# Queries and keys of batch 2: from pair loads and TensorE transposes to token rows and DMA transposes

## The chip, the cores and the metric

The kernel runs on one NeuronCore of a Trainium2 chip. A core has five engines with a queue of instructions each: TensorE (PE in the profile; its weight loads are PEld), VectorE (DVE), ScalarE (ACT), GpSimd (POOL) and SyncE (SP, which here only issues DMAs). Each queue runs in order, and an instruction waits until the semaphores that it names have been raised. Sixteen DMA engines move data between HBM and the on-chip memory SBUF; SyncE issues to the queue that the profile calls q1, GpSimd to q0. TensorE writes to PSUM[...].

The metric is the device time of one execution in microseconds; smaller is better.

## What is computed

```python
scores = q @ k.T / sqrt(64)                      # batch 8, heads 8, sequence 576, head 64
c      = cumsum(max(s, 0))                       # per batch and head
scores = where(causal, -1e9, scores + min(-(c[i] - c[j]), 0))
attn   = softmax(scores)
x      = (attn @ v), heads side by side          # 8 x 576 x 512
out    = x + relu(layernorm(x) * g @ w1) @ w2    # w1 512 x 2048, w2 2048 x 512
```

Inputs and the output are float32; the kernel multiplies in bf16.

## The kernel before

**The work.** Attention goes head by head: the loop over `n` runs over 64 heads, n = 8b + h for head h of batch b. One pass of it is called a slot here. In slot n TensorE computes the transposed scores of head n in three PSUM banks (`sa`, `sb`, `sc`, L312) and, in every second slot, the last 64 x 64 block of two heads (`sd`, L347); ScalarE takes their exponentials into `er` (L323, L358). Heads from n = 10 on (`NM`) are masked afterwards by GpSimd, four selects a head on the diagonal blocks of `er` (L331) and one for two heads on the last block (L361). One slot later comes `pv` of head n-1: 15 small matmuls into `pot` (L389), and VectorE's division and copy into `xb` (L397 to L406). Between these pieces stand the "units" of the layer norm and MLP of an earlier batch: `mlp1`, four matmuls into `ph` (L497), and `mlp2`, quarters of four matmuls into `py` (L515). In slots 9 to 15 there are two units a slot, in slot 16 four, from slot 20 on about four.

**Queries and keys, two ways.** The scores need q and k with the head dimension on the partitions, in the tile `kq[i]`, i = group mod 2. A group `gam` is four heads, so batch b has groups 2b and 2b + 1. Four more partition rows hold the bias: -1 and c (in three bf16 parts), against c and ones, so that the matmul of depth 68 adds the bias itself.

The *pair way* is for batches below `NPE`. Two heads form a pair. `ld_cast_pair` (L130) has GpSimd issue two loads with a cast into bf16 (`kp`, `qp`, L128). `qk_pair` (L275) then has TensorE transpose the pair, six 96 x 96 transposes for k and six for q into two PSUM tiles `trqk` of the pool `ps_t` (L255), which `sd` and others also use, and VectorE and ScalarE copy them into `kq` (L100, L98). `aug` (L207) writes the bias rows with four small DMAs from SyncE.

The *row way* is for the other batches. `ld_rows` (L159) loads 128 token rows of four heads in float32, k and q in one DMA each from SyncE (128 KB each, `rowtmp`, L164). `cast_rows` (L172) has GpSimd cast them into one of four tiles `rows` (L176) and copy the bias columns beside them from `cT` (L177). `tr_rows` (L182) has SyncE issue a DMA transpose of the tile into `kq` (L186). A group has five tiles, the last of 64 rows. `cT` holds the bias by tokens; `bias_rows` (L232) fills it at slot 9 from the PSUM tile `trc`, and two memsets put its constants in. In the row way's layout a matmul over queries that pass the 512th is cut in two (`q_cols`, L289).

**What sets the order.** The program is written out by hand (`tc.manual_schedule()`, L68): each engine's queue is in the order of the Python calls. At the start of slot n, `pre(n)` (L675) issues what is to be in time for later slots. For group `gam`, with m = n - 4 gam, rows 0 and 1 are loaded at m = -6, cast at -5 while rows 2 and 3 are loaded, transposed at -4 while rows 2 and 3 are cast and row 4 is loaded, and so on to the last transpose at -2; the group's first head is at m = 0. The values of batch 2 (`vtmp`, L139) are loaded by SyncE in slots 11 to 15 and cast by GpSimd a slot later (L102). As `pre(n)` stands ahead of the scores, GpSimd's casts of a slot stand ahead of that slot's selects in its queue. The loads share six buffers of the pool `stage`, so that SyncE can issue them ahead of the slot that they are written in. The weights `w1` and `w2` come through GpSimd's queue with a cast: `w2` is issued in slots 7 and 10 (L201).

Of the kernel before, what the change touches and what calls it, by code (L numbers as in the profile page):

```python
# [19 lines left out]
def kernel(  # L20
# [11 lines left out]
    nc = tc.nc  # L32
# [13 lines left out]
    EW = 1664  # L46
    G = 4
    NG = BH // G
    NPE = 3
    NM = 10  # L50
    NR = 4
    QT = 6
# [33 lines left out]
    cT = const.tile([P, NT, 2, BH, 4], BF16, name="cT")  # L86
# [39 lines left out]
    def ld_cast(kind, g):  # L126
        ready[kind, g] = pair_tile(kind)
        nc.gpsimd.dma_start(out=ready[kind, g][0:QP], in_=pair_src(kind, g))  # L128

    def ld_cast_pair(g):  # L130
        ld_cast("k", g)
        ld_cast("q", g)
# [12 lines left out]
    def ld_cast_v(b, t):  # L145
        pn = P if t < NF else TL
        nc.gpsimd.dma_start(
            out=v_bf[b % 2][:pn, t, :, 0:D],
            in_=v[b, :, t * P : t * P + pn, :].rearrange("h s d -> s h d"),
        )  # L150
# [8 lines left out]
    def ld_rows(gam, t):  # L159
        pn = P if t < NF else TL  # L160
        b, h0 = gam // 2, (gam % 2) * G
        tmp = stage.tile([P, 2, G, D], F32, name="rowtmp", tag="st")
        for u, src in enumerate((k, q)):
            nc.sync.dma_start(  # L164
                out=tmp[0:pn, u],
                in_=src[b, h0 : h0 + G, t * P : t * P + pn, :].rearrange("h s d -> s h d"),
            )
        loaded["rows", gam, t] = tmp
# [27 lines left out]
    def ld_w1(c):  # L196
        sl = slice(c * 512, (c + 1) * 512)
        nc.gpsimd.dma_start(out=w1_bf[:, :, sl], in_=w1_r[:, :, sl])

    def ld_w2(i):  # L200
        nc.gpsimd.dma_start(  # L201
            out=w2_bf[:, 4 * i : 4 * i + 4, :], in_=w2_r[:, 4 * i : 4 * i + 4, :]
        )
# [3 lines left out]
    def aug(gam, eng, h0=0):  # L207
        r = slice(gam * G + h0, gam * G + G)
        i = gam % 2
        eng.dma_start(out=kq[i][D : D + 1, 1, h0:G, 0:S], in_=c_hi[r, :])  # L210
        for j in range(3):
            eng.dma_start(out=kq[i][D + 1 + j : D + 2 + j, 0, h0:G, 0:S], in_=c3[r, j, :])
# [19 lines left out]
    def bias_rows(tr):  # L232
        for t0, t1, pn in ((0, NF, P), (NF, NT, TL)):
            nc.vector.tensor_copy(
                out=cT[0:pn, t0:t1, 0, :, 1:4],
                in_=tr[0:pn, :, t0:t1, :].rearrange("p j t x -> p t x j"),
            )
            nc.vector.tensor_copy(out=cT[0:pn, t0:t1, 1, :, 0], in_=tr[0:pn, 0, t0:t1, :])
# [42 lines left out]
    def k_cols(b, h, kb):  # L281
        i, hh = (b * 2 + h // G) % 2, h % G
        if b < NPE:
            return kq[i][0:KA, 0, hh, kb * P : (kb + 1) * P]
# [4 lines left out]
    def q_cols(b, h, q0, q1):  # L289
        i, hh = (b * 2 + h // G) % 2, h % G  # L290
        if b < NPE:
            return [(q0, q1, kq[i][0:KA, 1, hh, q0:q1])]
# [374 lines left out]
    keep_warm(5)  # L667

    PAIR_LOADS = {11: 8, 12: 9, 13: 10, 16: 11}
    PAIRS = {9: 5, 11: 6, 13: 7, 14: 8, 15: 9, 16: 10, 21: 11}


    def pre(n):  # L675
        if n == 0:
            nc.vector.memset(mhalf, -0.5)
            ld_cast_pair(4)
        elif n == 1:
            ld_w1(1)  # L680
        elif n == 3:
            ld_cast_pair(5)
            for t in range(NT):
                ld_cast_v(1, t)
        elif n == 4:
            ld_w1(2)
            ld_w1(3)
        elif n == 7:
            ld_cast_pair(6)
            ld_w2(0)  # L690
            ld_cast_pair(7)
            ld_w2(1)
        elif n == 10:
            ld_w2(2)
            ld_w2(3)
        elif n == 12:
            nc.vector.memset(cT[:, :, 0, :, 0], -1.0)
            nc.vector.memset(cT[:, :, 1, :, 1:4], 1.0)
        elif n == 16:
            for r in rows:  # L700
                nc.gpsimd.memset(r[:, :, :, KA:P], 0.0)
        if n in PAIR_LOADS:
            ld_cast_pair(PAIR_LOADS[n])
        if n % 4 == 0 and 2 <= n // 4 + 1 < 2 * NPE:
            aug(n // 4 + 1, nc.sync)
        for gam in range(2 * NPE, NG):
            m = n - 4 * gam
            if m == -6:
                ld_rows(gam, 0), ld_rows(gam, 1)
            elif m == -5:  # L710
                cast_rows(gam, 0), cast_rows(gam, 1)
                ld_rows(gam, 2), ld_rows(gam, 3)
            elif m == -4:
                tr_rows(gam, 0), tr_rows(gam, 1)
                cast_rows(gam, 2), cast_rows(gam, 3)
                ld_rows(gam, 4)
            elif m == -3:
                tr_rows(gam, 2), tr_rows(gam, 3)
                cast_rows(gam, 4)
            elif m == -2:  # L720
                tr_rows(gam, 4)
        for nb in range(2, B):
            m = n - H * nb + (5 if nb == 2 else 7)
            if 0 <= m < NT:
                ld_v(nb, m)
            if 1 <= m <= NT:
                cast_v(nb, m - 1, "pool")
# [17 lines left out]
    for n in range(BH):  # L745
        b, h = n // H, n % H
        pre(n)
        if n < 8:
            scores(b, h)
            if h in (1, 3, 5, 6):  # L750
                scores_d(b, h // 2)
            if h in (0, 2, 4):
                qk_pair(h // 2 + 1, ("dve", "dve"), ("act", "dve" if h < 4 else "act"))
            pend.append((b, h))
            if n == 7:
                pv_next()
                tr_pair(4)
                pv_next()
                evac_pair("k", 4, ("act", "act"))
                evac_pair("q", 4, ("act", "act"))  # L760
                trc = bias_tr()
                keep_warm(8)
                continue
            if n % 2 == 1 or n == 0:
                keep_warm(2)
            if n > 1:
                pv_next()
            if n == 6:
                pv_next()
            continue  # L770
        if n == 8:

            phs = [
                pool.tile([P, 512], F32, name="ph", tag=tag)
                for pool, tag in ((ps_m, "m"), (ps_m, "m"), (ps_s, "s"), (ps_s, "s"))
            ]

            def columns(t):
                cols = slice(t * P, (t + 1) * P)
                for fb, ph in enumerate(phs):  # L780
                    for kd in range(KD):
                        nc.tensor.matmul(  # L782
                            ph[:, cols],
                            lhsT=w1_bf[:, kd, fb * P : (fb + 1) * P],
                            rhs=xTs[0][:, kd, cols],
                            start=(kd == 0),
                            stop=(kd == KD - 1),
                        )

            for t in range(NF):  # L790
                ln_tr(0, t, "act" if t < 3 else "dve")
                if t > 0:
                    columns(t - 1)
            columns(NF - 1)
            for fb, ph in enumerate(phs):
                if fb % 2 == 0:
                    nc.scalar.activation(out=hT[:, fb, :], in_=ph, func=ACT.Relu)
                else:
                    nc.vector.tensor_scalar_max(out=hT[:, fb, :], in0=ph, scalar1=0.0)
            ln_first_rstd()  # L800
            queue += batch_units(0)[4:]
            scores(b, h)
            scores_d(b, h // 2)
            pend.append((b, h))
            run_units(1)
            continue

        end = next(m for m in (8 * i + 3 for i in range(2, B + 1)) if m >= n)
        nu = (2 if n < 16 else -(-len(queue) // (end - n + 1))) - 2
        if n in PAIRS:  # L810
            qk_pair(PAIRS[n], ("dve", "dve"), ("act", "act"))
        scores(b, h)
        run_units(1, True)
        if h % 2 == 0:
            scores_d(b, h // 2)
        run_units(1)
        if n > 9:
            pv_next()
        if n == 9:
            bias_rows(trc)  # L820
        pend.append((b, h))
        lt = {2: (0, 1), 3: (2, 3, 4)}.get(h, ()) if b > 1 else ()
        for t in lt:
            ln_tr(b - 1, t, "act" if b == 2 else "dve")
            if t != 1 and t != 4:
                run_units(1)
                nu -= 1
        if n == 2 * H + 2:
            for t in range(3, NT):
                ln_xn(1, t)  # L830
        run_units(nu)
        if b > 1 and h == 3:
            run_units(len(queue))
            queue += batch_units(b - 1)
# [41 lines left out]
```

## Time and profile before

| What | Before |
|---|---|
| Time, median of 3 runs | 368.11 us (367.84 to 368.29) |
| Span of the profiled execution | 367.0 us |
| Instructions | 8372 |
| TensorE busy | 357.8 us, 97% |
| VectorE busy | 205.8 us, 56% |
| ScalarE busy | 194.2 us, 53% |
| GpSimd busy | 161.3 us, 44% |
| SyncE's DMA queue (q1) | 40.74 MB, 50.9% of 16 engines |
| GpSimd's DMA queue (q0) | 8.62 MB, 20.4% of 16 engines |

A busy share is the time in which the engine had at least one instruction under way, over the span. The time line of an engine lists its instructions by start and length, with the idle time before one and what ended it in brackets. The window view of the DMA queues gives, for a stretch of time, how many packets and bytes each queue moved. DMA share and busy time say nothing of who waits; that is read from the brackets and from the starts.

Some starts in the time line that the steps ahead use (in us from the start of the span): `sa` of slots 10 to 17 at 42.87, 46.69, 49.54, 53.13, 56.48, 61.12, 64.48 and 69.43; `sa` of slot 24 at 100.87. The transposes of pairs 7 to 11 start at 52.62, 55.97, 60.30, 63.96 and 86.36.

### The profile page before, as it was taken

The numbers are of one execution on the slowest core, as the hardware profiler recorded it, in microseconds if no ns is written. First come the engines' busy times: TensorE is split into PE (matmuls) and PEld (weight loads), VectorE is DVE, ScalarE is ACT, GpSimd is POOL, SyncE is SP. The second block draws the span as 40 slices with busy tenths as digits, with TensorE's granted clock in tenths as the row PEclk, the third lists the DMA queues.
The fourth block names the chain that finished last, engine by engine and source line by source line (L and its number), as shares of the span: only waits on it lengthen the run. The fifth ranks groups of instructions, "written<-read, shape, count | busy, mean of one in ns | idle before, by whom it ended". The sixth has DMA issues, their size and how long they took to land.

```text
span 367.0 us, 8372 instructions
## 1 busy us (share of the span) xinstructions
PE 357.8 (97%) x3079; PEld 198.0 (54%) x3079; DVE 205.8 (56%) x539; ACT 194.2 (53%) x371; POOL 161.3 (44%) x441
## 2 busy tenths in 40 slices
PE   8899999999999999999999999999999999999995
PEld 3577565565555555555555555555555554444444
DVE  7597789796438453944384547743675483112211
ACT  5795988568743674357534753476337522501410
POOL 8864375747553746445754562555652101000000
PEclk9999999999999999999999999999999999999999
DMA  7999995579965989599968996798730011011013
GB/s 138 170 195 175 201 204 88 116 179 173 187 140 129 236 177 189 117 227 184 192 158 203 206 188 133 183 202 183 167 102 2 0 60 57 3 56 58 3 29 86
DMA packets 147981, 50.42 MB, mean 137 GB/s; under 512 B 134185, under 2 KB 143268, under 8 KB 147940
## 3 DMA queue, kind: packets, MB, share of 16 engines
q1 hardware_dynamic: 129364, 40.74, 50.9%
q0 software_dynamic: 18176, 8.62, 20.4%
q10 hardware_dynamic: 400, 0.52, 0.5%
q8 instruction: 24, 0.39, 0.4%
q14 instruction: 17, 0.14, 0.2%
HBM read 37.11 MB, written 9.44 MB: 127 GB/s over the span
## 4 chain that ended last, share of the span: by engine, by line
PE 85%; DVE 7%; ACT 3%; DMA 2%; issue 1%; ACTq 0%
PE ph L497 32%; PE py L515 31%; PE pot L389 7%; PE sc L312 4%; PE sa L312 3%; PE sb L312 3%; DVE xn L451 2%; PE trx L484 2%; ACT er L323 2%; DMA kq<-c 1%; ACT kq L98 1%; PE trqk L255 1%; DVE stats L423 1%; PE ph L782 1%; DMA c_in<-in_s_dram 1%
## 5 line engine op out<-in xcount | busy, mean ns | idle before, releaser
L515 PE MATMUL py<-w_bf,hT 128*128 128x512 bf16 (+1 forms) x592 | 136.5, 373 | 0.4 <-DVE yo L524 0.4
L497 PE MATMUL ph<-xT,w_bf 128*128 128x512 bf16 x496 | 117.8, 379 | 0.1
L507 ACT ACTIVATE hT<-ph 128x512 bf16<-128x512 f32 x102 | 61.0, 598 | 62.8 <-PE ph L497 62.8
L515 PEld LDWEIGHTS <-hT 128*128 128x128 bf16 x592 | 53.5, 98 | 49.1 <-issue 0.9
L497 PEld LDWEIGHTS <-w_bf 128*128 128x128 bf16 x560 | 50.3, 97 | 51.7 <-issue 3.3
L323 ACT ACTIVATE er<-sa 128x512 bf16<-128x512 f32 x64 | 38.2, 597 | 70.3 <-PE sa L312 39.9
L331 POOL TENSOR_SCALAR_AFFINE_SELECT er<-er 128x128 bf16<-128x128 bf16 x216 | 58.2, 294 | 26.4 <-ACT er L323 26.3
L505 DVE TENSOR_SCALAR hT<-ph 128x512 bf16<-128x512 f32 x38 | 26.3, 692 | 54.5 <-PE ph L497 49.1
L176 POOL CAST rows<-rowtmp 128x512 bf16<-128x512 f32 (+1 forms) x50 | 30.5, 609 | 49.1 <-DMA rowtmp<-in_q_dram 48.4
L312 PEld LDWEIGHTS <-kq 68*128 68x128 bf16 x440 | 32.8, 97 | 26.5 <-DMA kq<-c 1.6
L389 PEld LDWEIGHTS <-er 128*128 128x128 bf16 x960 | 37.4, 98 | 14.2 <-issue 0.7
L389 PE MATMUL pot<-v_bf,er 128*128 128x65 bf16 x960 | 39.6, 193 | 0.1
L323 ACT ACTIVATE er<-sc 128x512 bf16<-128x512 f32 x64 | 39.1, 610 | 0.0
L397 DVE RECIPROCAL rinv<-pot 128x5 f32<-128x5 f32 x64 | 12.3, 192 | 47.5 <-PE pot L389 47.2
L323 ACT ACTIVATE er<-sb 128x512 bf16<-128x512 f32 x64 | 38.3, 598 | 0.1
L524 DVE SCALAR_TENSOR_TENSOR yo<-py,rstd,xb 128x512 f32<-128x512 f32 x32 | 23.9, 748 | 25.5 <-PE py L515 20.8
L399 DVE TENSOR_TENSOR xb<-pot,rinv 128x256 f32<-128x256 f32 x64 | 27.2, 425 | 2.2
L439 POOL TENSOR_TENSOR rstd<-rstd,mhalf 128x4 f32<-128x4 f32 (+1 forms) x8 | 8.8, 1097 | 43.8 <-DVE rstd L438 43.8
L312 PE MATMUL sa<-kq 68*128 68x512 bf16 x64 | 24.4, 381 | 1.2 <-DMA kq<-c 1.1
L423 DVE BATCH_NORM_STATS2 stats<-xb 128x6 f32<-128x128 f32 (+2 forms) x100 | 25.3, 312 | 0.4
L312 PE MATMUL sc<-kq 68*128 68x256 bf16 (+1 forms) x208 | 25.2, 232 | 0.3
L102 POOL CAST v_bf<-vtmp 128x512 bf16<-128x512 f32 (+1 forms) x30 | 18.4, 613 | 14.3 <-DMA vtmp<-in_v_dram 14.3
(101 smaller groups left out, 332.8 us busy)
## 6 DMA issues: line engine op xcount, KB each, us to landing
out_dram<-yo SPq DMA_DIRECT2D x32, 256.0 KB
vtmp<-in_v_dram SPq DMA_DIRECT2D x24, 256.0 KB
rowtmp<-in_k_dram SPq DMA_DIRECT2D x40, 128.0 KB
rowtmp<-in_q_dram SPq DMA_DIRECT2D x40, 128.0 KB
w_bf<-in_moe_w_ch_dram POOLq DMA_DIRECT2D x8, 512.0 KB, 11.1
kp<-in_k_dram POOLq DMA_DIRECT2D x11, 144.0 KB, 6.6
qp<-in_q_dram POOLq DMA_DIRECT2D x11, 144.0 KB, 7.3
v_bf<-in_v_dram POOLq DMA_DIRECT2D x8, 128.0 KB, 8.5
```

The source lines that it names most:

```text
L176: nc.gpsimd.tensor_copy(out=r[0:pn, :, :, 0:D], in_=loaded.pop(("rows", gam, t))[0:pn])
L312: nc.tensor.matmul(a[:, c + a0 - q0 : c + a1 - q0], lhsT=k_cols(b, h, kb), rhs=cols, start=True, stop=not (pe_mask and diag),)
L323: nc.scalar.activation(out=e[:, o : o + 512], in_=a, func=ACT.Exp, scale=scale)
L331: nc.gpsimd.affine_select(out=e[:, o : o + P], in_=e[:, o : o + P], compare_op=ALU.is_ge, fill=0.0, base=0, pattern=[[1, P]], channel_mult ...
L389: nc.tensor.matmul(pot[:, t, :], lhsT=e[:, o : o + P], rhs=vv[:, kb, h, :], start=(kb == 0), stop=(kb == last),)
L399: nc.vector.tensor_tensor(out=xb[b][:, :, hs], in0=pot[:, 0:NF, 0:D], in1=rinv[:, 0:NF].unsqueeze(2).to_broadcast([P, NF, D]), op=ALU.mult,)
L423: nc.vector.bn_stats(out=st[b][:, t, part, :], in_=x[:, lo:hi])
L497: nc.tensor.matmul(ph, lhsT=w1_bf[:, kd, fb * P : (fb + 1) * P], rhs=xT[:, kd, :], start=(kd == 0), stop=(kd == KD - 1),)
L505: nc.vector.tensor_scalar_max(out=hT[:, fb, :], in0=ph, scalar1=0.0)
L507: nc.scalar.activation(out=hT[:, fb, :], in_=ph, func=ACT.Relu)
L515: nc.tensor.matmul(py[0], lhsT=hT[:, fb, t * P : (t + 1) * P], rhs=w2_bf[:, fb, c0:c1], start=(fb == 0), stop=(fb == FB - 1),)
L524: nc.vector.scalar_tensor_tensor(out=yo, in0=py[0], scalar=rs, in1=x[:, c0:c1], op0=ALU.mult, op1=ALU.add)
```

## The change

Batch 2 goes from the pair way to the row way. `NPE` is 2 in place of 3, so that groups 4 and 5 come from `ld_rows`, `cast_rows` and `tr_rows` in slots 10 to 18, and scores of batch 2 read the row layout. Pairs 8 to 11 go from the tables of loads and transposes; pairs 5 to 7 stay, with loads in slots 3 and 7 that the diff doesn't touch. The two `aug` calls of groups 4 and 5 (slots 12 and 16) drop out by the bound on `n // 4 + 1`. As `cast_rows` now needs `cT` in slot 11, its two memsets come ahead of `bias_rows` in slot 9, and the zeroing of the four tiles `rows` moves from slot 16 to slot 10. The purpose is to take batch 2's transposes from TensorE and their evacuations from VectorE and ScalarE, and to use the DMA path that batches 3 to 7 already have.

```diff
-    NPE = 3
+    NPE = 2
...
-    PAIR_LOADS = {11: 8, 12: 9, 13: 10, 16: 11}
-    PAIRS = {9: 5, 11: 6, 13: 7, 14: 8, 15: 9, 16: 10, 21: 11}
+    PAIRS = {9: 5, 11: 6, 13: 7}
...
         elif n == 10:
             ld_w2(2)
             ld_w2(3)
-        elif n == 12:
-            nc.vector.memset(cT[:, :, 0, :, 0], -1.0)
-            nc.vector.memset(cT[:, :, 1, :, 1:4], 1.0)
-        elif n == 16:
             for r in rows:
                 nc.gpsimd.memset(r[:, :, :, KA:P], 0.0)
-        if n in PAIR_LOADS:
-            ld_cast_pair(PAIR_LOADS[n])
...
         if n == 9:
+            nc.vector.memset(cT[:, :, 0, :, 0], -1.0)
+            nc.vector.memset(cT[:, :, 1, :, 1:4], 1.0)
             bias_rows(trc)
```

## The prediction

> **What bounds the kernel now.** I read the shares first, then the chain that ended last, then the time line of slots 12 to 16 engine by engine, then the DMA queues by window. A slot is one head, n = 8b+h; its scores start with the `sa` matmul.
>
> ```profile
> PE 357.8 (97%) x3079; PEld 198.0 (54%) x3079; DVE 205.8 (56%) x539; ACT 194.2 (53%) x371; POOL 161.3 (44%) x441
> ...
> PE 85%; DVE 7%; ACT 3%; DMA 2%; issue 1%; ACTq 0%
> ```
>
> TensorE is the bound, so a change pays by what it takes from TensorE's queue and costs what it makes that queue wait for. In the time line, TensorE's part of slots 13 to 15:
>
> ```profile
> 52.87 0.42 PE L255 MATMUL trqk<-ident,qp 96*128 96x96 bf16 x6
> 53.13 0.38 PE L312 MATMUL sa<-kq 68*128 68x512 bf16 x1
> ...
> 55.51 0.62 PE L389 MATMUL pot<-v_bf,er 128*128 128x65 bf16 x15
> 55.97 0.42 PE L255 MATMUL trqk<-ident,kp 96*128 96x96 bf16 x6
> 56.22 0.42 PE L255 MATMUL trqk<-ident,qp 96*128 96x96 bf16 x6
> 56.48 0.38 PE L312 MATMUL sa<-kq 68*128 68x512 bf16 x1
> ...
> 58.56 0.22 PE L347 MATMUL sd<-kq 68*128 68x64 bf16 x2 [0.40 <-ACT kq L98]
> ```
>
> The 12 transposes of a pair take 0.51 us (55.97 to 56.48), and their evacuation then holds up `sd`. The `pot` at 55.51 is PV of head 12; it needs that head's four causal selects (L331), which GpSimd issues in order behind the casts of the same slot:
>
> ```profile
> 52.52 1.04 POOL L331 TENSOR_SCALAR_AFFINE_SELECT er<-er 128x128 bf16<-128x128 bf16 x4
> 53.52 0.29 POOL L361 TENSOR_SCALAR_AFFINE_SELECT er<-er 64x128 bf16<-64x128 bf16 x1
> ...
> 55.23 0.61 POOL L102 CAST v_bf<-vtmp 128x512 bf16<-128x512 f32 x1 [0.19 <-DMA vtmp<-in_v_dram]
> ```
>
> So head 12's selects end at 53.6, 1.9 us before PV wants them, and a cast at the head of GpSimd's queue does wait for its DMA. Last, the queues in 34 to 40 us, when SyncE's queue (q1) holds one load, the values of batch 2, tile 0, issued at 30.30:
>
> ```profile
> DMA packets 2000, 1.17 MB, mean 195 GB/s; under 512 B 1013, under 2 KB 1999, under 8 KB 1999
> q0 software_dynamic: 1034, 0.90, 91.5%
> q1 hardware_dynamic: 965, 0.25, 30.8%
> ```
>
> That one load of 256 KB, 1024 packets of 256 B, needs those six microseconds: while GpSimd's queue (q0: weights, pairs) has a backlog, the queues get packets one for one, and q1's are small.
>
> [...] Here the window 86 to 102 us, six transposes among row loads, moved this much[...]:
>
> ```profile
> DMA packets 11261, 2.84 MB, mean 177 GB/s; under 512 B 11256, under 2 KB 11256, under 8 KB 11257
> ```
>
> [...]
>
> **The change part by part.**
>
> *TensorE work removed.* Pairs 8 to 11 (slots 14, 15, 16, 21): 4 x 0.51 = 2.05 us. Their waits go too: slot 14 lasts 3.82 us from `sa` to the next transposes, against 3.08 for slot 12, which has no pair: 0.74. In slot 15 the transposes take 0.82, not 0.51: 0.31. In slot 16 `sd` comes 1.20 us after the first unit starts, against 0.86 in slot 12: 0.34. Sum 3.44 us. The eight evacuations on DVE and eight on ACT (0.80 each) lie beside TensorE and pay only through those waits.
>
> *TensorE work added.* Batch 2's scores take the split layout, three more small matmuls a head. From `sa` to the next unit it is 0.65 us in slot 16 (pair layout, 64.48 to 65.13) and 0.66 in slot 24 (row layout): 8 x 0.01, nothing.
>
> *DVE, two memsets at slot 9.* 0.33 + 0.86 us ahead of `bias_rows`. PV of head 9 waits for its bank and comes at 45.73; `bias_rows` ended at 44.77, so 1.2 us more would reach about 46.0: up to 0.2 us, taken as 0.1.
>
> *GpSimd.* The four row memsets (1.81 us) move to slot 10, where GpSimd idled 3.05 us: nothing. Eight pair issues at 0.64 go (5.1 us); ten casts at 0.61 and ten bias copies at 0.21 come (8.2 us). It is 44% busy; busy time is not the cost, waiting is.
>
> *The new wait.* After the two old `aug` calls SyncE's next instructions are the rows of group 4, tiles 0 to 3: eight loads, 4 x 1024 packets, issued from 30.3 on, ahead of the values. They meet the same backlog. From 34 to 49 us q0 moved 1034 + 1931 = 2965 packets (second number: window 40 to 49). Shared at 172 a us (1034/6) those last to 34 + 17.2 = 51.2. Meanwhile q1 gets 161 a us: 2770 packets. Left are 1326 of rows and 1024 of values. Alone, q1 moved 11257 packets in 16 us, 704 a us: 3.3 us, to 54.5. From last packet to release I take 1.4 us (the completions of the load issued at 30.30 end at 41.7, its packets near 40.3): 55.9. Cast 0.6, four selects 1.04: head 12's selects end at 57.6, later if the slowest of the 16 engines lags. PV wants them at 55.5: a wait of 2.1 us or more.
>
> Behind that, each slot's selects stand behind the cast of the next load, and q1 carries transposes too (a 128-row tile 1024 packets, like its load). At 704 a us: two transposes, the half tile and values 1 (3584 packets) end at 59.6, so head 13's selects at 62.6; TensorE, 3.1 us after its last PV began (0.46 + 2.63 as in slot 12), asks at 60.7: 1.9. Two transposes and values 2 (3072) end at 64.0, selects at 67.0; asked at 65.4 (0.46 + 2.38 as in slot 13): 1.6. Half a transpose, two tiles of group 5 and values 3 (3584) end at 69.1, selects at 72.1; asked at 70.1: 2.0. The next slots are longer and GpSimd catches up. Sum 7.6 us. All five transposes of group 4 land by about 66, when slot 16 starts near 67.5: no wait of their own.
>
> *Both ends of the unknown rate.* Row loads alone can run near the pace at which SyncE issues them, 512 packets in 0.51 to 0.56 us, some 950 a us. The same steps then give waits of 1.2, 0.7, 0.4 and 0.7: 3.0 us. At 600 a us, below any such window here, they give 2.7, 2.8, 2.3 and 2.9: 10.7 us. I take 704, since transposes are in the mix, and that slowest engine is not in it.
>
> *Removed at no gain.* Pair loads leave q0 after 49 us, when w2 is nearly in; two `aug` calls, eight small DMAs, were in time already.
>
> Net: -3.4 + 0.1 + 7.6 = +4.3; shaded for a rate above 704 where loads alone are queued, +4: 372.0 us.
>
> **The rivals.**
> 1. *The rows come in time* and TensorE keeps all 3.4 us: 364.7. For it: in batches 3 to 7 the same path starves GpSimd for 48.4 us of waits for rows, yet TensorE is at 9 tenths nearly throughout. Against it: slots 22 to 24 last 4.6 us each, slots 11 to 15 3.6 on average (46.69 to 64.48), and q0 is empty there.
> 2. *Waits and savings cancel*: the 950 end, 368.1 - 3.4 + 3.0 = 367.7, or up to 368.5. For it: loads in isolation run at that pace. Against it: five transposes in the stretch.
> 3. *Worse*: at 600 a us, 368.1 - 3.3 + 10.7 = 375.5[...]: taken as 376.5. [...]
>
> **How the numbers follow.** Forecast 0.60, rival 1 0.17, rival 2 0.10, rival 3 0.13. The range runs from below rival 2, 366.5, to 377.5, leaving out rival 1 and the far end of rival 3. Faster by over 0.2% (under 367.4): rival 1 and a little of rival 2, 0.19. Within 0.2%: 0.05. Slower: 0.76.
>
> **What would show it.** No `trqk` after slot 13; q1 holding 4 x 1024 row packets in 34 to 54 us at one for one with q0; GpSimd's L176 waiting for `rowtmp` in 50 to 56 us; head 12's selects after 56.5; gaps on TensorE ahead of `pot` L389 in slots 13 to 16, put down to POOL `er` L331. I am wrong if L331 of head 12 ends before 55.5: then the sharing of the queues was misread and rival 1 holds.

## The result and the profile after

The changed kernel takes 372.41 us (median; 371.49 to 372.76), the kernel before 368.20 us beside it: a ratio of 1.0108, 95% interval 1.0083 to 1.0133. It is slower, by about 4.2 us.

The page of the kernel after, its lines for the shares, the DMA engines in 40 slices, the two queues and the chain that ended last:

```profile
PE 359.1 (97%) x3055; PEld 196.9 (53%) x3055; DVE 200.4 (54%) x531; ACT 188.4 (51%) x363; POOL 168.6 (45%) x453
...
DMA  8999999999997999689988989699730011011013
...
q1 hardware_dynamic: 148372, 45.43, 58.4%
q0 software_dynamic: 16512, 7.44, 17.1%
...
PE 63%; DMA 15%; SPq 8%; DVE 6%; POOL 4%; issue 2%; ACT 1%; POOLq 0%; ACTq 0%
```

TensorE has 24 matmuls fewer (48 transposes of pairs out, 24 small score matmuls in) and yet is "busy" for longer; its clock, at half for 3.4 us, explains that below. The line that tells the story is the last: DMA and SyncE's queue (SPq) hold 23% of the chain of work that ended last, where DMA held 2% before.

Where the 4 us lie is read from the starts of `sa`, slot by slot. The column "bare" is a run that is told of further down, without the rows of group 4.

| Slot length, us | before | after | bare |
|---|---|---|---|
| 10 | 3.82 | 4.58 | 4.59 |
| 13 | 3.35 | 2.84 | 2.84 |
| 14 | 4.65 | 3.93 | 3.07 |
| 15 | 3.35 | 5.27 | 2.84 |
| 16 | 4.96 | 7.86 | 4.63 |
| 20 | 5.14 | 4.63 | 4.63 |
| 21 | 4.81 | 4.57 | 4.57 |
| 24 | 4.63 | 5.04 | 4.63 |
| 10 to 24 together | 62.64 | 66.70 | 59.75 |

From 62.64 to 66.70 is +4.06, about the difference of the two profiled executions (spans of 367.0 and 371.1 us). The slots between that are not listed agree within 0.02. Outside these slots two small differences nearly cancel: this execution came to slot 10 by 0.69 us sooner, in a start that differs from execution to execution, and lost 0.6 us after slot 24.

What the change spares is 3.65: 62.64 - 59.75 = 2.89, and 0.76 more because slot 10 is longer. What it costs is 0.76 in slot 10 and 66.70 - 59.75 = 6.95 in slots 14, 15, 16 and 24.

TensorE's time line, after (start, length, engine, line, operation, and in brackets the idle time before it and what ended it):

```profile
45.79 0.63 PE L389 MATMUL pot<-v_bf,er 128*128 128x65 bf16 x15 [0.57 <-DVE cT L238]
...
58.94 1.20 PE L389 MATMUL pot<-v_bf,er 128*128 128x65 bf16 x15
59.98 0.38 PE L312 MATMUL sa<-kq 68*128 68x512 bf16 x1
...
64.03 1.11 PE L389 MATMUL pot<-v_bf,er 128*128 128x65 bf16 x15 [1.50 <-POOL er L331]
65.25 0.38 PE L312 MATMUL sa<-kq 68*128 68x512 bf16 x1
67.01 0.57 PE L312 MATMUL sb<-kq 68*128 68x64 bf16 x3 [1.39 <-DMA kq<-rows]
...
67.83 1.90 PE L515 MATMUL py<-w_bf,hT 128*128 128x512 bf16 x4
```

From slot 10 on the `pot` of slot n is PV of head n - 2: slots 8 and 9 add their heads to the list and run no PV, so the lag is two slots and not the one that the description of the kernel before gives. The `pot` at 58.94 and at 64.03 are those of heads 12 and 13.

Read the lengths too. A `pot` of 15 matmuls takes 0.6 us; those at 58.94 and 64.03 take 1.2 and 1.1, because the selects that they wait for come one by one while it runs, and that part of the wait stands in no bracket. The four `py` matmuls at 67.83 take 1.90 in place of 1.03: half the clock, which this line of the view by windows shows (the PEclk is the third figure from the end; it was 1.00 in the windows on both sides):

```profile
67.10:70.50 3.40, 3.40 (x16) 1.52 (x17) 0.82 (x2) 1.36 (x3) 2.73 (x9) 0.50 1.01 228
```

By estimate, 3.40 us at a clock of 0.50 cost 1.7 us, and no idle time is to be seen: TensorE counts as busy for all 3.40. A run that is told of further down, with the clock at full (run 2), bears this out: from `sb` of slot 16 to `sa` of slot 17 it takes 4.42 us there (66.53 to 70.95) and 6.09 here (67.01 to 73.10).

GpSimd's time line, after, says why the selects are late:

```profile
53.84 0.61 POOL L176 CAST rows<-rowtmp 128x512 bf16<-128x512 f32 x1 [3.04 <-DMA rowtmp<-in_q_dram]
...
56.31 0.61 POOL L176 CAST rows<-rowtmp 128x512 bf16<-128x512 f32 x1 [1.71 <-DMA rowtmp<-in_q_dram]
...
58.03 0.62 POOL L102 CAST v_bf<-vtmp 128x512 bf16<-128x512 f32 x1 [0.95 <-DMA vtmp<-in_v_dram]
58.59 1.04 POOL L331 TENSOR_SCALAR_AFFINE_SELECT er<-er 128x128 bf16<-128x128 bf16 x4
...
63.12 0.61 POOL L102 CAST v_bf<-vtmp 128x512 bf16<-128x512 f32 x1 [0.91 <-DMA vtmp<-in_v_dram]
63.68 1.03 POOL L331 TENSOR_SCALAR_AFFINE_SELECT er<-er 128x128 bf16<-128x128 bf16 x4
```

Three casts wait for their DMA, and head 12's selects, which need none of these data, stand behind them: they end at 59.6 (53.6 before). Head 13's stand behind the cast of values 1, at 63.12, and end at 64.7. The DMA queues of the kernel after in 34 to 51 us, and then in 51 to 73:

```profile
q0 software_dynamic: 2828, 2.57, 90.9%
q1 hardware_dynamic: 2829, 0.70, 31.5%
```

```profile
q1 hardware_dynamic: 15358, 3.82, 91.7%
q0 software_dynamic: 356, 0.34, 9.2%
```

In 34 to 51 us, while w2 has a backlog, it is one packet for one (2829 of q1, 2828 of q0), and q1 gets 0.70 MB against 2.57. In 51 to 73 us q1 moves 15358 packets, 698 a us in the mean, but not evenly. The share of the DMA engines in this stretch, in 40 slices of 0.55 us, is in the first line that of the kernel after, in the second that of the kernel before:

```profile
DMA  9999986599416994454999997999799999999998
...
DMA  7999999999999953000000000000000599999943
```

Before, the engines stand idle for some 8 us of it. After, they are busy but for gaps near 57 and from 59 to 61.5 us; from 58 to 74 us q1 moves 13040 packets, 815 a us. Around those gaps SyncE's time line has

```profile
49.22 8.92 SPq L186 DMA_TRANSPOSE kq<-rows  x2
...
59.63 0.61 SPq L139 DMA_DIRECT2D vtmp<-in_v_dram  x1
```

The first two transposes hold SyncE for 8.92 us, and the load of values 1 is issued behind them, at 59.63.

### The profile page after: what moved, and what is told of

Its sections match the earlier page's. It is cut to its first block, busy times and chain, and to the rows that moved or that the text cites. A ratio compares the mean times of both kernels' runs of the same rounds, so it can differ in the third digit from the quotient of the medians.

```text
span 371.1 us, 8359 instructions
## 1 busy us (share of the span) xinstructions
PE 359.1 (97%) x3055; PEld 196.9 (53%) x3055; DVE 200.4 (54%) x531; ACT 188.4 (51%) x363; POOL 168.6 (45%) x453
## 3 DMA queue, kind: packets, MB, share of 16 engines
q1 hardware_dynamic: 148372, 45.43, 58.4%
## 4 chain that ended last, share of the span: by engine, by line
PE 63%; DMA 15%; SPq 8%; DVE 6%; POOL 4%; issue 2%; ACT 1%; POOLq 0%; ACTq 0%
PE py L515 26%; PE ph L497 23%; SPq L164 6%; DMA rowtmp<-in_q_dram 6%; PE pot L389 5%; DMA kq<-rows 3%; DMA vtmp<-in_v_dram 3%; PE sb L312 2%; PE sc L312 2%; PE sa L312 2%; DVE xn L451 2%; POOL er L331 1%; DMA kq<-c 1%; PE trx L484 1%; POOL rows L176 1%
## 5 line engine op out<-in xcount | busy, mean ns | idle before, releaser
L515 PEld LDWEIGHTS <-hT 128*128 128x128 bf16 x592 | 53.6, 98 | 49.6 <-issue 2.1
L331 POOL TENSOR_SCALAR_AFFINE_SELECT er<-er 128x128 bf16<-128x128 bf16 x216 | 60.8, 307 | 17.5 <-ACT er L323 17.5
L176 POOL CAST rows<-rowtmp 128x512 bf16<-128x512 f32 (+1 forms) x60 | 36.7, 612 | 65.1 <-DMA rowtmp<-in_q_dram 61.9
L312 PEld LDWEIGHTS <-kq 68*128 68x128 bf16 x464 | 34.0, 98 | 29.4 <-DMA kq<-rows 3.3
L389 PEld LDWEIGHTS <-er 128*128 128x128 bf16 x960 | 37.6, 98 | 17.8 <-POOL er L331 2.6
L389 PE MATMUL pot<-v_bf,er 128*128 128x65 bf16 x960 | 40.8, 194 | 2.3 <-POOL er L331 1.5
L397 DVE RECIPROCAL rinv<-pot 128x5 f32<-128x5 f32 x64 | 12.3, 193 | 53.3 <-PE pot L389 53.0
L312 PE MATMUL sb<-kq 68*128 68x384 bf16 (+2 forms) x176 | 24.7, 244 | 2.0 <-DMA kq<-rows 1.6
```

The source lines that it names most:

```text
L176: nc.gpsimd.tensor_copy(out=r[0:pn, :, :, 0:D], in_=loaded.pop(("rows", gam, t))[0:pn])
L312: nc.tensor.matmul(a[:, c + a0 - q0 : c + a1 - q0], lhsT=k_cols(b, h, kb), rhs=cols, start=True, stop=not (pe_mask and diag),)
L331: nc.gpsimd.affine_select(out=e[:, o : o + P], in_=e[:, o : o + P], compare_op=ALU.is_ge, fill=0.0, base=0, pattern=[[1, P]], channel_mult ...
L389: nc.tensor.matmul(pot[:, t, :], lhsT=e[:, o : o + P], rhs=vv[:, kb, h, :], start=(kb == 0), stop=(kb == last),)
L515: nc.tensor.matmul(py[0], lhsT=hT[:, fb, t * P : (t + 1) * P], rhs=w2_bf[:, fb, c0:c1], start=(fb == 0), stop=(fb == FB - 1),)
```

## The experiments

Each run changes the changed kernel, unless it says otherwise; a ratio is to the kernel before, measured beside it (368.13 us beside runs 1 to 4, 368.41 beside 5 to 7 and 10, 368.22 beside 8 and 9). Theory A is that of the prediction: the data come late because the DMA queues are full, and the waits of TensorE only pass this on; each expectation says what follows from it in that run.

**1. The constants sooner.** `cT`'s constants and the zeroes of `rows` are written by GpSimd in slot 8.

```diff
+        elif n == 8:
+            nc.gpsimd.memset(cT[:, :, 0, :, 0], -1.0)
+            nc.gpsimd.memset(cT[:, :, 1, :, 1:4], 1.0)
+            for r in rows:
+                nc.gpsimd.memset(r[:, :, :, KA:P], 0.0)
```

> The changed kernel, with the two memsets of cT and the four of rows put on GpSimd in slot 8, where it waited 4.5 us for the statistics. Theory A (DMA data of group 4 come late; the memsets only cost the 0.57 us that PV waits for the bank of trc in slot 10): the wait in slot 10 goes and the time falls by 0.5 to 0.8 us, to about 371.7. Theory B (the later waits have slack of their own and swallow it, since the DMA chain sets slots 14 to 16 by absolute time): slot 10 is shorter by 0.7 us, but slots 14 to 16 are longer by as much, and the time stays at 372.4.

Measured: 373.31 us, ratio 1.0142 (1.0122 to 1.0161), above what either theory gave; of the two, theory B of this run is the nearer. Slot 10 is back to 3.82 us, so its 0.76 us were the memsets. But their removal bought nothing: slots 15 and 16 take 4.01 and 9.14 us. `sa` of slot 17 starts at 73.63, against 73.10 after, although TensorE reached slot 16 sooner:

```profile
64.49 0.38 PE L312 MATMUL sa<-kq 68*128 68x512 bf16 x1 [0.23 <-DMA kq<-rows]
...
66.21 0.61 PE L312 MATMUL sb<-kq 68*128 68x64 bf16 x3 [1.34 <-DMA kq<-rows]
```

The last transposes still land when slot 16 has begun. The clock was then halved (PEclk 0.50) for two windows, 65.6 to 72.4, in place of one, which made it worse than after. (This profile comes to slot 10 by 2.1 us later than the one after, and it had a halved window earlier too, PEclk 0.50 in 14.4 to 17.8 us; its starts are to be read with that in mind.)

**2. TensorE kept busy.** Seven matmuls on zeroes go ahead of PV in slot 15 and ahead of the scores in slot 16, where it waited.

```diff
+        if n == 16:
+            keep_warm(7)
...
+        if n == 15:
+            keep_warm(7)
```

> The changed kernel, with seven idle matmuls of 512 columns (1.5 us) ahead of PV in slot 15 and seven ahead of the scores of slot 16, where TensorE waits anyway. Theory A (1.7 us of the loss is the halved clock after these waits): the granted clock stays at 1.0 and the time falls by 1.5 to 2 us, to about 370.6. Rival (the half clock is hidden behind the DMA chain, or comes from elsewhere): the time stays at 372.4 or rises by up to 3 us of idle matmuls.

Measured: 372.66 us, ratio 1.0118 (1.0104 to 1.0132): theory A's 370.6 missed, the rival's 372.4 came. The clock stays full (a mean of 1.0 in the profiled execution, 0.995 after), slot 16 takes 5.17 us, and `sa` of slot 17 comes at 70.95, 2.15 us sooner than after. Then it is given back, wait by wait:

```profile
78.17 0.74 PE L389 MATMUL pot<-v_bf,er 128*128 128x65 bf16 x10 [0.43 <-POOL er L331]
...
85.28 0.38 PE L312 MATMUL sb<-kq 68*128 68x64 bf16 x3 [0.45 <-DMA kq<-rows]
...
104.93 0.40 PE L312 MATMUL sb<-kq 68*128 68x64 bf16 x3 [1.09 <-DMA kq<-rows]
```

At slot 25 it is 0.5 us behind after. So in this run the full clock alone buys nothing: what it gains comes back as waits for selects and for `kq`. That the packets of the DMA queues make these later waits was not shown.

**3. Half of w2.** The second half of `w2` is not loaded, and the first half is used twice (the output is then not that of the reference).

```diff
-            ld_w2(2)
-            ld_w2(3)
...
-                rhs=w2_bf[:, fb, c0:c1],
+                rhs=w2_bf[:, fb % 8, c0:c1],
```

> The changed kernel without the loads of the second half of w2, its first half used twice (that part of the computation is left out). 1 MB, 1024 packets of GpSimd's queue, are taken out of the backlog in which the rows of group 4 are loaded. Theory A (the DMA engines are full from the start to 74 us, and the rows get one packet for each packet of GpSimd's queue): group 4's rows land by 50 us, the waits of slots 14 to 16 go or fall below 1 us in all, and the time is 364.5 to 367. Rival (GpSimd's 8 us of added casts and copies, or the DMA transposes themselves, make the waits): 371 to 372.4.

Measured: 365.87 us, ratio 0.9944 (0.9933 to 0.9955). Nothing of the row path was touched, and all its waits up to slot 23 are gone. GpSimd's line for the selects of head 12, which end at 53.3 as before the change:

```profile
52.25 1.04 POOL L331 TENSOR_SCALAR_AFFINE_SELECT er<-er 128x128 bf16<-128x128 bf16 x4
```

`sa` of slot 17 starts at 66.12, 6.98 us sooner than after; 0.49 of this was there at slot 11. This is theory A. In the profiled execution about half is lost again at slot 24 (8.18 us in place of 4.63), where TensorE, now early, waits for group 6 and drops to half the clock (two windows of the kernel with half of w2, the second with PEclk 0.50). That execution is the slowest of 20, 368.64 us with a mean clock of 0.994; the other 19 have 0.998 or more, so the halved window is its own:

```profile
98.96 0.39 PE L312 MATMUL sb<-kq 68*128 68x64 bf16 x3 [1.73 <-DMA kq<-rows]
```

```profile
96.60:100.00 3.40, 1.67 (x13) 0.77 (x12) 0.34 (x2) 1.81 (x5) 1.85 (x6) 1.00 1.21 127
100.00:103.40 3.40, 3.40 (x25) 1.84 (x23) 0.00 (x0) 0.81 (x3) 2.35 (x8) 0.50 1.37 219
```

**4. Rows for group 5 alone.** Group 4 keeps its pairs, so that the first rows are wanted four slots later.

```diff
+    NPG = 5
...
-        if b < NPE:
+        if b * 2 + h // G < NPG:
...
-    PAIRS = {9: 5, 11: 6, 13: 7}
+    PAIR_LOADS = {11: 8, 12: 9}
+    PAIRS = {9: 5, 11: 6, 13: 7, 14: 8, 15: 9}
```

> Half of the change: group 4 stays on the pair way, group 5 takes the row way (loads from slot 14 on). Theory A (only the loads that meet the backlog of GpSimd's queue cost; group 5's come after it): no wait for rows or casts on TensorE, pairs 10 and 11 with their waits saved (about 1.6 us), 0.7 us lost to the memsets in slot 9: 367.0 to 367.6 us. Rival (the row way costs GpSimd or DMA time in itself): half of the loss, about 370.

Measured: 367.68 us, ratio 0.9979 (0.9963 to 0.9996): slightly faster than before, just above theory A's span. No wait for rows is left in slots 10 to 24; slot 10 keeps its 0.58 us for `cT`. Group 5's rows cost TensorE nothing; group 4's, asked for in the stretch of w2, do.

**5. The selects ahead of the casts.** Before slot 20 GpSimd casts a slot's rows and values after the slot's selects.

```diff
+    late = []
+    def behind(n, f, *a):
+        if n < 20:
+            late.append(lambda: f(*a))
...
-                cast_rows(gam, 0), cast_rows(gam, 1)
+                behind(n, cast_rows, gam, 0), behind(n, cast_rows, gam, 1)
```

> The changed kernel, but for slots before 20 GpSimd gets the casts of rows and values behind the slot's causal selects in place of ahead of them. Nothing is loaded sooner. Theory A (the row data is late because the DMA queues are full from 34 to 73 us; GpSimd's order only passes the lateness on): the waits for selects in slots 14 and 15 go (0.84 and 2.43 us), but the transposes of group 4 can't start sooner, so that slot 16 takes the lateness over as one wait of its sb for kq of 3 to 5 us, with the clock halved behind it: sa of slot 17 at 72 to 74 (after: 73.10), time 371.5 to 373.5. Rival C (the lateness is made by GpSimd's queue, in which selects stand behind a cast that waits): the waits of slots 14 and 15 go and nothing takes their place, 369 to 370.

Measured: 373.29 us, ratio 1.0113 (1.0077 to 1.0149), as theory A said (`sa` of slot 17 at 74.44, a little past its 72 to 74). TensorE's PV no longer waits, and the scores of slot 16 do, for longer:

```profile
62.12 0.62 PE L389 MATMUL pot<-v_bf,er 128*128 128x65 bf16 x15
...
65.50 0.38 PE L312 MATMUL sa<-kq 68*128 68x512 bf16 x1 [2.76 <-DMA kq<-rows]
...
67.14 0.60 PE L312 MATMUL sb<-kq 68*128 68x64 bf16 x3 [1.26 <-DMA kq<-rows]
```

The last transpose lets `sb` go at 67.14; after, it was 67.01. GpSimd's order decides in which bracket the wait stands, not how long it is in all.

**6. The rows of group 4 sooner.** Tiles 0 to 3 are loaded in slot 5.

```diff
+        elif n == 5:
+            ld_rows(4, 0), ld_rows(4, 1), ld_rows(4, 2), ld_rows(4, 3)
```

> The changed kernel with the first four row tiles of group 4 loaded in slot 5 in place of slots 10 and 11, some 20 us sooner, ahead of the long stretch of w2. Theory A (the same bytes must pass by 73 us, whatever their order, if the queues are full all the way): the first row wait is gone, but the transposes and values then still end near 64 to 67, so that no more than 1 to 2.5 us come back: 370 to 371.5. Rival D (only the order of the loads is wrong, and q1 has idle time before 34 us that takes them): slots 14 to 16 lose all their waits, 372.4 - 6.5 to 7 = 365.5 to 366.

Measured: 372.06 us, ratio 1.0103 (1.0059 to 1.0147). Its four executions are far apart: two took 371.09, inside theory A's span, the profiled one among them, the others 373.04 and 375.07. Rival D is out in any case. The casts of the four tiles wait no more, and the next tile is as late as ever, in GpSimd's time line at 61.62 (61.45 after):

```profile
61.62 0.60 POOL L176 CAST rows<-rowtmp 64x512 bf16<-64x512 f32 x1 [7.79 <-DMA rowtmp<-in_q_dram]
```

What q1 got sooner, q0 lost. In 24 to 34 us q1 moved 3197 packets (178 after) and q0 4745 (5786 after); the last of `w2` landed at 58.0 in place of 55.5, and until then it shared the engines with the first transposes. The queues of this run in 51 to 58 us, with q0 still at work where it was nearly done after:

```profile
q0 software_dynamic: 846, 0.83, 70.5%
q1 hardware_dynamic: 1483, 0.37, 59.9%
```

**7. Half of w2 later.** It is issued in slot 12.

```diff
         elif n == 10:
-            ld_w2(2)
-            ld_w2(3)
...
+        elif n == 12:
+            ld_w2(2)
+            ld_w2(3)
```

> The changed kernel with the second half of w2 issued by GpSimd in slot 12 in place of slot 10, some 7 us later. Theory A, sharing: one packet for one, q0's backlog ends sooner for the first rows, but the 2 MB of w2 then meet the transposes. The row waits of slots 14 and 15 fall by 1 to 2 us and what lies behind takes back half: 370.5 to 372. If only the one-for-one sharing in 34 to 51 us counts (rival E), the gain is the whole of what the rows were held up, as with half of w2 not loaded up to slot 23: 366 to 368.

Measured: 372.81 us, ratio 1.0112 (1.0079 to 1.0144): no gain, above theory A's span, though its upper end is within the noise, and a miss for rival E. The first rows came in time (slot 14 takes 3.09 us), and then the weights met values 1 and the transposes: that load landed at 63.1, just as after. TensorE waited once for selects, for longer, and then 1.31 us for `kq` at `sb` of slot 16, with the clock at half (PEclk 0.50) from 63.9 to 70.7:

```profile
64.10 1.26 PE L389 MATMUL pot<-v_bf,er 128*128 128x65 bf16 x15 [2.47 <-POOL er L331]
```

Runs 6 and 7 change the order in both directions, and `sa` of slot 17 starts within some 1 us of the same time (72.08 and 73.31, 73.10 after). In these runs what has to pass decides, not when each piece was asked for.

**8. No rows for group 4.** Its loads, casts and transposes are left out; heads 16 to 19 take what group 2 left in `kq`, in the pair layout, so the output is not that of the reference.

```diff
-        if b < NPE:
+        if b * 2 + h // G < 5:
...
-        for gam in range(2 * NPE, NG):
+        for gam in range(2 * NPE + 1, NG):
```

> The changed kernel without any work for the rows of group 4: no load, no cast, no transpose; heads 16 to 19 take the queries, keys and bias of group 2, which are still in the buffer, in the pair layout. What TensorE is spared by the change is kept in full and nothing of group 4 has to come through the queues: this is rival 1 of the prediction made real. By the waits of the trace after, slots 14 to 16 become 3.08, 2.84 and 4.82 us in place of 3.93, 5.27 and 7.86: 6.3 less, and 372.4 - 6.3 = 366.1; 366 to 366.8 if slot 24 keeps its wait. If the slots stay long (rival C, GpSimd's order or TensorE's own queue as the cause), over 368.

Measured: 365.57 us, ratio 0.9928 (0.9910 to 0.9946). This is the column "bare" of the table: 2.65 us under the kernel before, which is what the slots say (2.89) within 0.25. What TensorE was to be spared is really there, and it is the rows of this one group that take it back, 6.95 us.

**9. Rows without transposes.** The loads and casts of group 4 stay, its five transposes go; heads 16 to 19 are fed as in run 8.

```diff
-                tr_rows(gam, 0), tr_rows(gam, 1)
+                gam > 4 and (tr_rows(gam, 0), tr_rows(gam, 1))
```

> The changed kernel without the five DMA transposes of group 4; its rows are loaded and cast as before, and heads 16 to 19 take the queries, keys and bias of group 2 in the pair layout. It parts the loads from the transposes. Theory A: head 12's selects still wait for the row loads, which meet w2 (slot 14 keeps its 0.84 us), but values 1 and the half tile no longer queue behind two transposes of some 1.5 us each: slot 15 keeps 0 to 0.7 of its 2.43 us, and slot 16 nothing, since neither a late transpose nor a halved clock is left: 372.4 - 2 - 3 = 367.0 to 368. If the loads are the whole of it (rival F), slots 14 and 15 stay as after and only slot 16 gains: 369.2 or more.

Measured: 365.76 us, ratio 0.9934 (0.9913 to 0.9955), below the 367.0 to 368 of theory A: the loads cost less than it gave them. Here TensorE waits only inside the PV of head 12 (0.88 us long in place of 0.62; slot 14 takes 3.35 us):

```profile
58.75 0.88 PE L389 MATMUL pot<-v_bf,er 128*128 128x65 bf16 x15
...
61.85 0.62 PE L389 MATMUL pot<-v_bf,er 128*128 128x65 bf16 x15
```

So of the 6.95 us the loads alone make 0.28, and 6.7 us need the transposes too, by estimate 1.7 of it as the halved clock (PEclk 0.50 for 3.4 us). They are 4608 packets, by estimate 5.7 us of a full queue at the 815 a us of 58 to 74 us. Yet full engines are not all of it: without the transposes of group 4 q1 moves even more packets in 51 to 67 us, 11246 against 10100 after, and TensorE hardly waits (0.28 us, as above), as these are loads that are needed later.

For head 13 the traces say where the time went. Values 1 are issued at 55.66 in this run (the line holds values 2 too):

```profile
55.66 1.79 SPq L139 DMA_DIRECT2D vtmp<-in_v_dram  x2
```

They landed at 59.6, 3.9 us later (GpSimd's cast of values 1, at 60.03, had nothing to wait for); after, they were issued at 59.63 and landed at 63.1, 3.4 us later. The load itself was not slower, it was issued 4.0 us later, behind two transposes. Whether these hold SyncE so long by their packets or by something else about their issue, the runs don't part, and no run issues values 1 ahead of them.

**10. A version that beats both.** Group 5 alone by rows, with `cT`'s constants written by GpSimd in slot 8.

```diff
+        elif n == 8:
+            nc.gpsimd.memset(cT[:, :, 0, :, 0], -1.0)
+            nc.gpsimd.memset(cT[:, :, 1, :, 1:4], 1.0)
```

> Only group 5 (heads 20 to 23) goes the row way, group 4 stays with pairs, and the two constant memsets go to GpSimd in slot 8, ahead of their use, in place of VectorE in slot 9. Theory A: the run with group 5 alone by rows gave 367.68; the wait of 0.58 us for cT in slot 10 goes: 367.0 to 367.2, faster than both kernels. Rival: as the wait of slot 10 is taken back further on, as in the run with constants early, 367.7.

Measured: 366.66 us, ratio 0.9946 (0.9926 to 0.9965), 1.75 us under the kernel before, and some 5.7 under the changed one (measured apart). Slot 10 takes 3.84 us, slots 15 and 16 take 2.84 and 4.82. Here what the sooner constants gain is kept: no later slot waits for rows and takes it back. The chain of this kernel is as short of DMA as before the change:

```profile
PE 85%; DVE 6%; ACT 3%; POOL 2%; DMA 2%; issue 1%; POOLq 0%; ACTq 0%
```

## Why the prediction was right, and where its steps were off

The time, the direction and the cause held: 372.0 forecast, 372.4 measured, by a row path that meets w2 one packet for one and hands its lateness to TensorE through GpSimd's casts. Runs 3, 8 and 9 show the cause by taking w2's second half, the rows or the transposes away; run 5 shows that GpSimd's order only passes it on. Of the signs named ahead, no `trqk` after slot 13, the one for one, the casts that wait for `rowtmp` and the late selects of head 12 came; the waits of `pot` came in slots 14 and 15 alone. That the sum came out so close was luck: only 3.29 us of the 6.95 came through the casts, and terms that its sum didn't hold made up the rest.

- **What is spared**: 3.44 forecast, 3.65 measured (run 8). Right; the 0.2 more is slot 21, which took 4.81 before and 4.57 without pair 11.
- **The memsets**: "up to 0.2 us, taken as 0.1". Wrong in size: 0.76. Set against the start of `sa` of slot 10, `bias_rows` ended 1.65 us later than before, not 1.2: VectorE's time line has the memsets' 0.33 and 0.86, and 0.39 of idle time ahead of the first. The slack was 0.96; the rest, 0.69, is most of the 0.76, with the wait of `pot` at 45.79 (PV of head 8, not 9). In run 1 it went with the memsets.
- **The sharing**: 2829 packets of q1 beside 2828 of q0 by 51 us, as forecast (2770). But the backlog of q0 was to end at 51.2, and w2's last piece landed at 55.5; 356 of q0's packets came after 51. The backlog was counted to 49 us of the kernel before, where w2 landed only at 52.2. So head 12's selects ended at 59.6, not 57.6, and head 13's at 64.7, not 62.6. The rate after it, 704 forecast, was 698 in the mean of 51 to 73 us, by a mix of gaps and of 815 a us from 58 on.
- **Who asks when**: the step that failed. "PV wants them at 55.5" and "TensorE ... asks at 60.7" take PV as one slot behind; from slot 10 on it is two. Head 12 was asked for in slot 14, at 58.9, head 13 in slot 15, near 62.5. The four waits of 2.1, 1.9, 1.6 and 2.0 were in truth two, 0.86 and 2.43 (what slots 14 and 15 are over those of run 8), and in slots 16 and 17 none. PV and the data were both put too early, by 3.4 and 2.0 us for head 12, so that the errors cancelled in part: 3.29 us of waits in PV in place of 7.6.
- **"All five transposes of group 4 land by about 66 ...: no wait of their own"**: wrong. The last landed at 67.0, one us late, but slot 16 had started at 65.25 and not at 67.5, since the waits ahead of it were smaller than forecast; `sb` waited 1.39 us.
- **The halved clock** has no place in the sum of 7.6 us. It came (PEclk 0.50 from 67.1 to 70.5) and cost, by estimate, 1.7 us, behind waits of 1.5 and 1.4 us.
- **Slot 24** was not looked at: 0.41 us for `kq`.

Together: 7.6 us of waits forecast, all in PV; 6.95 came, 3.29 in PV, 3.23 in slot 16 (by estimate 1.7 of it as a slow clock) and 0.41 in slot 24. Group 5's rows are free, as rival 1 had it for both groups (runs 4 and 10); group 4's are not.

## What to carry to other kernels

Before moving work to DMA, count the packets that must pass in the stretch up to the moment of need, of all queues together, and add the new ones; look also at what stands ahead of a needed load in the queue of the engine that issues it. In this kernel neither an earlier or later issue nor another order on GpSimd helped (runs 5 to 7), only fewer packets or a later need (runs 3, 4 and 9). A wait that was removed alone (runs 1, 2 and 5) came back at the next instruction that needed the late data. And check the lag of a software pipeline in the code: a wait is only as long as the time by which the consumer asks ahead of the data.

## What the runs showed of the hardware

**The clock at half** came for one or two windows of 3.4 us, behind waits of TensorE. In the kernel after, the granted clock was 0.50 from 67.09 to 70.50 us and 1.00 on both sides. Read in windows of 3.40 us, it was 0.50 for one window in run 6 (65.9 to 69.3) and for two in a row in runs 1, 5 and 7 (from 65.6, 66.3 and 63.9). In the window just ahead, still at 1.00, TensorE was busy for 1.55 of 3.41 us (45%, after), 1.41 of 3.40 (41%, run 6), 1.13 (33%, run 7), 0.38 (11%, run 5), 1.67 (49%, run 3) and even 2.30 (68%, run 1). But windows of 2.26 of 3.42 (66%, after) and 2.38 of 3.40 (70%, run 6) were followed by one at 1.00. Near the start of run 1 a window of 1.89 (56%) was followed by one at half. In the kernel after it came behind waits of 1.5 and 1.4 us; these windows show no sharp limit. At half, a window with TensorE busy for 2.79 of 3.40 us (82%, run 1), 2.56 (75%, run 5) or 1.88 (55%, run 7) was followed by another at half; in the kernel after, with 3.40 of 3.40, it was followed by one at 1.00, and in run 6 the one with 3.17 (93%) was the only one, by the execution's mean clock of 0.995.

**DMA transposes** ended 1.04 us apart when two stood in the queue (64.07 and 65.11 in the kernel after), no slower than a tile's two loads: behind another transpose, which ended at 66.97, four row loads of 512 packets of 256 B ended at 67.65, 68.42, 68.90 and 69.49, 0.63 us apart in the mean. By estimate a transpose is 1024 packets: over the whole execution the change put 19008 packets more on q1 (148372 against 129364), and 9 tiles with 1024 each for loads and for transposes make 18432. At 256 B each that is 256 KB in 1.04 us, 252 GB/s, in a queue with other work. Fast as it is, a transpose is not free: it puts 1024 packets beside the 1024 of the tile's loads.

**SyncE's issues took longer in the stretch of w2**: in the kernel after, a row load's issue took 0.5 to 0.6 us in 65 to 69 us, but 2.3 to 3.5 us in 31 to 46 us, and two transposes took 8.92 us from 49.22 on but 2.68 us from 60.40 on. All later loads stand behind that. That the length comes from loads that had not yet passed is likely, and not tested.
